# Pair 7's transposes in the other half of a PSUM pair, eight slices of an output tile ahead of pair 6's second scores, and nine more fixed orders, in a cosine attention with a gated product behind it

## The chip, the cores and the metric

The kernel runs on one core of a Trainium2 chip. Its engines are TensorE (PE, the matmuls), VectorE (DVE), ScalarE (ACT), GpSimd (POOL) and SyncE (SP, which here only issues transfers). Each engine works through its own list of instructions in order and waits at semaphores for the others. The metric is the device time in microseconds (us), the median of some runs. Beside it stands one profiled execution, whose rows give each instruction's start and length counted from the start of its span.

## The reference

The inputs are `q`, `k` and `v` of shape (8, 12, 448, 64): batch, heads, positions, width of a head; then `w_in` (768, 2048) and `w_out` (2048, 768), and the scale `tau` = 0.1. Cut to what matters:

```python
q_n = q / (norm(q, axis=-1) + 1e-06)
k_n = k / (norm(k, axis=-1) + 1e-06)
scores = q_n @ k_n.T / tau                       # 448 x 448 for each batch and head
attn = exp(scores - max); attn = attn / (sum(attn) + 1e-09)
attn_out = attn @ v
x = attn_out.transpose(0, 2, 1, 3).reshape(3584, 768)
h = x @ w_in                                     # 3584 x 2048
g = h * cos(h)
out = g @ w_out                                  # 3584 x 768
```

## The kernel before

**How the work is cut.** Two heads make a *pair* `g` (48 of them), three pairs a *unit* `u` (16), two units a batch `b` (8). Six pairs give the 768 columns of `x` for one batch of 448 rows.

For a unit, `load` brings q and k. `square` (`sq4.2` is unit 4, pair 2 of the unit) and `reduce` (`red4.2`, on DVE) give squared norms, `rnorm` their inverse roots, `scale` the normalised q and k in `qks`. `transposes(g)` turns them into `qkT`. From pair 9 on that is a transposing transfer issued on SP (`T39` is pair 39's). Before that it is seven PE transposes in two parts (`TP6`), written to PSUM, and one DVE copy (`qkT6`, L716). There are three `qkT` buffers.

`scores(g, c)` computes one of four chunks (`SC7.1` is pair 7, chunk 1; chunk 0 is half as long as the others) into `SC1` for even c and `SC0` for odd c, and ACT takes the exponential into `PX` (`exp7.1`, L742). So a score has to wait until the exponential two chunks earlier has emptied its buffer. `attend` multiplies by v into the PSUM pair AV (`AV7`, with a rest `R7` for the half chunk). Row sums come from ones in the same product for the "direct" pairs (among them 7 to 11 and 17), or for the others from `counts` (`S6`, L788), which marks the sums into AV; a DVE copy (`xs2`) and a small chain of transfers (gather, reciprocal, spread, bcast) bring the inverse sums back. `xa` and `xb` are the DVE copies that empty AV. The last step for a pair is `x7`, the product with the inverse sums, on POOL for all pairs from 6 on.

With a batch's six pairs in `xT`, `m1(b)` computes h in 16 passes of six matmuls (`M1 0.13` is batch 0, pass 13, L953). Two passes fill one PSUM pair; ACT takes the cosine (`sin0.6`, L982) and DVE the product (`g0.6`, L984) into `gT`. The cosine and the exponential need different ACT tables, so a table load (L556) stands between. For batch 0 the eight pairs of passes go to the PSUM pairs MP, SC1's pair, SC0's, AV and so on by `"first": (3, 1, 2, 0, 3, 1, 2, 0)`, counted in AV, SC0, SC1, MP. Passes 8 and 9 are thus in MP, 12 and 13 in the PSUM pair `SC[1]`, 14 and 15 in AV.

The second product works on output tiles of 128 rows (28 of them). Its units here are *slices*: one slice takes 128 of the 2048 inner columns for half of the 768 output columns; a tile has 32. While attention still runs, a slice is done as four 64 by 64 matmuls into both halves of MP (`m2_quarters`, L1053). The first tile takes its slices in runs (0 to 8, 8 to 12, 12 to 16, each with both crossings, `"cuts": (8, 12)`), and a run on the other crossing waits until the last has drained. Slices 0 to 7 need the parts W2.0 and W2.1 of `w_out`, 8 to 11 W2.2, 12 to 15 W2.3. `osb10` is the copy of tile 10 out of PSUM, by DVE for one half and ACT for the other, and `out10` its store.

**The halves of MP.** The PSUM pair MP has two banks: the lower is `TP` (and `TPF` for the second product), the upper `PO` or, in bfloat16, `POT`. In `transposes`, pairs in `PLAN["other"]` would use `POT`; the others use `TP`.

**How the pairs and the second product are woven.** `pair(g, f)` issues pair g's four scores, pair g-1's attend, and between them slices of the second product, as many as the four numbers `f` say: `f[0]` after the first score, `f[1]` and `f[2]` around the third, `f[3]` after the fourth. Pair 6 takes `f` from `PLAN["six"]`; the others from `PLAN["given"]` where they stand there, or from `shares`. For pairs whose predecessor is in `PLAN["quarters"]`, `f[1]` stands before the attend of that predecessor.

**What sets the order.** Each step is an `Op` with an engine, what it reads and writes, and a cost that the plan assumes. `Program.arrange` (L152) plays the list three times: PE keeps nearly the order written (it may pick among the next 8, or 24 at the start), the other engines pick, of what is ready, the step with the earliest due time, worked back from when PE needs it. `emit` (L315) then writes each engine's list with its waits. Near the end of the program `PLAN["then"]` is read (L1326):

```python
for x, y in PLAN["then"]:
    P.order_only([o for o in P.ops if o.label == x and o.eng == find(y).eng][-1], find(y))
```

which makes step y stand behind step x on y's engine. It adds no wait between engines.

Of the kernel before, what the change touches and what calls it, by code (L numbers as in the profile page):

```python
# [35 lines left out]
    "split5at": 0,  # L36
    "wait6": 1,
    "b5": -5.0,
    "then": [('g5.0', 'recip12'), ('g5.6', 'red15.2'), ('osb10', 'ln11.0'), ('xa32', 'red12.1'), ('sq12.2', 'x29'), ('g5.7', 'red15.2'), ('xa37', 'red14.1'), ('sq7.1', 'scale6.1'), ('g2.7', 'red9.1'), ('T20', 'out4')],
    "u7": (None, None, None),  # L40
    "v6": "sq5.1",
    "yield": {},
# [7 lines left out]
    "turned": 9,  # L50
    "first": (3, 1, 2, 0, 3, 1, 2, 0),
    "inner": {6: (6, 7), 7: (8,)},
    "other": (),
    "bs": -1.0,
    "cuts": (8, 12),
    "bx": 0.0,
    "six": (0, 8, 4, 4),
    "cycle": {13: 3, 14: 3, 15: 3, 16: 3, 17: 3, 18: 3, 46: 3, 47: 3},
    "quarters": (7, 8, 9, 10, 11, 17),
    "turns": {3: (3, 0, 1, 2, 0, 1, 2, 0)},  # L60
# [5 lines left out]
    "u5": ("gather2", "gather2", "gather2"),  # L66
    "tail": 192,
    "twin": 4,
    "given": {13: (0, 0, 3, 3), 16: (5, 1, 3, 6), 22: (0, 3, 5, 6), 26: (3, 2, 5, 6), 27: (0, 0, 3, 2), 34: (12, 4, 5, 6), 46: (12, 4, 4, 5), 47: (3, 1, 5, 0), 14: (4, 0, 3, 3), 15: (3, 1, 4, 2), 17: (2, 1, 3, 4), 18: (3, 0, 3, 4), 19: (6, 4, 2, 7), 20: (0, 5, 5, 3), 21: (3, 5, 3, 6), 23: (4, 1, 5, 5)},
    "roots": (3, (8, 0), (10, 0), (12, 0), (14, 0)),  # L70
    "lead": {33: 5, 45: 5, 12: 13, 21: 13},
    "vloads": {3: [(4, "x6"), (5, "x6")], 4: [], 5: [], 6: [(7, "x15"), (8, "x15")], 7: [], 8: [], 9: [], 10: [], 11: [], 12: [], 13: []},
# [1292 lines left out]
```

## Time and profile before

| | |
|---|---|
| median of 3 runs | 415.38 us (415.3 to 415.99) |
| the profiled execution | 415.07 us, span 413.2 us |
| PE busy | 404.6 us (98%) |
| ACT busy | 270.2 us (65%) |
| POOL busy | 248.6 us (60%) |
| DVE busy | 199.8 us (48%) |
| granted TensorE clock | 1.0 of full speed |

The span is the time from the first to the last profiled instruction; the execution's own time is 1.9 us longer. In a row of the timeline the first number is the start and the second the length, then engine, line, operation, what is written from what is read, and the count; in square brackets stands the idle time of the engine before it and who ended it. Matmuls overlap, so a row of several can be longer than its share of PE's time, and the distance between starts tells the work.

### The profile page before, as it was taken

What the parts mean: (1) busy time and instruction counts of PE and PEld (TensorE: products, weight loads), DVE (VectorE), ACT (ScalarE), POOL (GpSimd) and SP (SyncE); (2) the same over time, 40 slices, a digit from 0 to 9 for tenths busy, and PEclk for the clock granted to TensorE, in tenths of its full rate; (3) what the DMA queues carried; (4) which work ended last, traced back from release to release, by engine and by line L of the source; (5) the groups of instructions that cost most, each with busy time, mean ns of one, the idle gap of its engine ahead of it and who ended that gap; (6) DMA issues with size and microseconds to landing.
All of it is one profiled execution on the core that took longest, in us unless ns stands there. A gap on an engine that the chain in (4) does not pass through costs nothing.

```text
span 413.2 us, 13911 instructions
## 1 busy us (share of the span) xinstructions
PE 404.6 (98%) x6213; PEld 244.0 (59%) x6213; DVE 199.8 (48%) x279; ACT 270.2 (65%) x384; POOL 248.6 (60%) x196
## 2 busy tenths in 40 slices
PE   7899999999999999999999999999999999999997
PEld 3454556655566655765567656865567655655565
DVE  4574653426664457445644567344652344413421
ACT  4897578985889645985497647884488745623500
POOL 4999995894776975988589756946456303011000
PEclk9999999999999999999999999999999999999999
DMA  8999999589989999587978975797746531151023
GB/s 183 249 254 226 207 223 200 134 158 215 180 147 171 234 260 189 98 195 182 208 120 189 250 128 110 137 236 167 104 89 108 147 84 33 47 139 38 2 74 80
DMA packets 78736, 63.99 MB, mean 155 GB/s; under 512 B 41844, under 2 KB 72404, under 8 KB 78676
## 3 DMA queue, kind: packets, MB, share of 16 engines
q1 hardware_dynamic: 60468, 50.42, 55.0%
q0 software_dynamic: 18048, 12.59, 20.8%
q8 instruction: 49, 0.80, 0.8%
q10 hardware_dynamic: 160, 0.10, 0.1%
q14 instruction: 11, 0.09, 0.1%
HBM read 55.44 MB, written 11.19 MB: 161 GB/s over the span
## 4 chain that ended last, share of the span: by engine, by line
PE 91%; POOL 3%; ACT 2%; DVE 2%; DMA 1%; issue 0%; SPq 0%; ACTq 0%; POOLq 0%
PE MP L1053 27%; PE SC L953 20%; PE AV L953 12%; PE SC L727 6%; PE AV L764 5%; PE MP L1082 4%; PE AV L788 4%; PE SC L1082 3%; PE MP L953 2%; PE AV L837 2%; POOL qks L678 1%; PE SC L735 1%; ACT cosb L982 1%; PE MP L852 1%; PE AV L1082 1%; DMA raw<-in_q_dram 1%
## 5 line engine op out<-in xcount | busy, mean ns | idle before, releaser
L742 ACT ACTIVATE PX<-SC 128x448 bf16<-128x448 f32 (+1 forms) x192 | 148.9, 825 | 15.9 <-PE SC L727 10.5
L1053 PE MATMUL MP<-W,gT 64*64 64x384 bf16 x2816 | 136.6, 323 | 0.8 <-DVE qkT L716 0.6
L1053 PEld LDWEIGHTS MP<-W,gT 64*64 64x64 bf16 x2816 | 80.0, 107 | 34.9 <-issue 4.4
L953 PE MATMUL SC<-xT,W 128*128 128x448 bf16 x444 | 90.9, 353 | 0.0
L678 POOL TENSOR_TENSOR qks<-raw,rn 128x896 bf16<-128x896 f32 (+1 forms) x48 | 79.9, 1677 | 13.0 <-ACT rn L670 12.6
L640 POOL TENSOR_TENSOR sq<-raw 128x896 bf16<-128x896 f32 x44 | 74.0, 1687 | 12.4 <-DMA raw<-in_q_dram 7.7
L940 POOL TENSOR_TENSOR xT<-xu,RB 128x448 bf16<-128x448 f32 x36 | 40.2, 1136 | 66.1 <-DMA RB<-scr 66.1
L953 PEld LDWEIGHTS SC<-xT,W 128*128 128x128 bf16 x444 | 43.1, 98 | 40.2 <-issue 0.4
L982 ACT ACTIVATE cosb<-SC,cst 128x896 f32<-128x896 f32 x37 | 37.2, 1006 | 37.8 <-PE SC L953 35.9
L953 PE MATMUL AV<-xT,W 128*128 128x448 bf16 x276 | 59.6, 352 | 0.0
L984 DVE TENSOR_TENSOR gT<-SC,cosb 128x896 bf16<-128x896 f32 x37 | 40.3, 1089 | 29.2 <-ACT cosb L982 29.1
L647 DVE TENSOR_REDUCE n<-sq 128x14 f32<-128x896 bf16 (+2 forms) x49 | 51.4, 1058 | 6.1 <-ACT sq L638 4.9
L727 PE MATMUL SC<-qkT 64*64 64x448 bf16 x576 | 51.9, 354 | 0.3
L982 ACT ACTIVATE cosb<-AV,cst 128x896 f32<-128x896 f32 x23 | 23.2, 1007 | 37.1 <-PE AV L953 35.4
L774 DVE COPY xu<-AV 128x448 f32<-128x448 f32 x36 | 22.5, 624 | 49.1 <-PE AV L756 49.1
L953 PEld LDWEIGHTS AV<-xT,W 128*128 128x128 bf16 x276 | 26.6, 98 | 25.4 <-DVE xs L799 1.1
L984 DVE TENSOR_TENSOR gT<-AV,cosb 128x896 bf16<-128x896 f32 x23 | 25.1, 1089 | 27.4 <-ACT cosb L982 27.4
L764 PE MATMUL AV<-PX,va 64*64 64x448 bf16 x432 | 38.2, 349 | 0.0
L614 POOL DMA_DIRECT2D va<-in_v_dram x32 | 22.0, 694 | 24.8 <-DVE gT L984 20.2
L1019 DVE COPY osb<-MP 128x384 f32<-128x384 f32 x26 | 14.5, 557 | 43.1 <-PE MP L1053 32.0
L727 PEld LDWEIGHTS SC<-qkT 64*64 64x64 bf16 x576 | 16.8, 106 | 12.8 <-ACT PX L742 5.9
L775 DVE TENSOR_TENSOR xu<-xu,AV 128x448 f32<-128x448 f32 x36 | 22.3, 621 | 1.2
(84 smaller groups left out, 364.1 us busy)
## 6 DMA issues: line engine op xcount, KB each, us to landing
raw<-in_k_dram SPq DMA_DIRECT2D x48, 224.0 KB, 5.2
raw<-in_q_dram SPq DMA_DIRECT2D x48, 224.0 KB, 5.6
out_dram<-osb SPq DMA_DIRECT2D x54, 192.0 KB, 3.4
RB<-scr SPq DMA_DIRECT2D x22, 336.0 KB, 5.3
va<-in_v_dram POOLq DMA_DIRECT2D x32, 192.0 KB, 6.9
W<-in_moe_w_in_dram POOLq DMA_DIRECT2D x4, 768.0 KB, 14.8
W<-in_moe_w_out_dram POOLq DMA_DIRECT2D x4, 768.0 KB, 18.9
qkT<-qks SPq DMA_TRANSPOSE x39, 3.8
```

The lines of the kernel that those rows point to most:

```text
L640: pool(lambda e, x=x, y=y: e.tensor_tensor(y, x, x, ALU.mult), src_, dst, 0.1 + n * 1.78e-3, label="sq%d.%d" % (u, p)).pad = LATE if u > 1 ...
L647: dve(lambda e, w=w: e.tensor_reduce(out=n2v[i][:, 2 * p : 2 * p + 2, w], in_=sqv[p][:, :, w, :], axis=mybir.AxisListType.X, op=ALU.add), ...
L678: f = lambda e, s0=s0, s1=s1: e.tensor_tensor(qksv[i][:, p, s0:s1].rearrange("p s h d -> p h s d"), rawv[i][:, h, s0:s1, :], bass.AP(rn[i] ...
L727: m = e.matmul(SCv[z][BP * o : BP * o + BP, a, 0:S], t[r, c - 1 + (NT3 + 1) * o, 0:BP], t[r, :, BP : 2 * BP], start=True, stop=True)
L742: act(lambda e: e.activation(PHv[j] if c == 0 else PXv[j][:, c - 1], SCv[z][:, :, 0:n], ACT.Exp, scale=1.0 / TAU), ["SC%d" % z], [("PX", j ...
L764: m = e.matmul(AVv[64 * a : 64 * a + 64, o, 0:S], vav[y][r, 2 * p + a, c + 1, :], PXv[j][r, c, a, :], start=(c == 0), stop=False)
L940: f = lambda e, p=p: e.tensor_tensor(xTv[b % 2][:, UP * i + p, :].rearrange("p (s o m) -> p o s m", s=NB, o=2), xuv[:, u % 3, p, :].rearra ...
L953: t = e.matmul(ph[:, a, 0:S], W1v[:, order[c], 128 * n : 128 * n + 128], xTv[b % 2][:, order[c], :], start=(c == 0), stop=(c == NKC - 1))
L982: act(lambda e, ph=ph, cz=cz: e.activation(cosv[cz], ph[:, :, 0:S], ACT.Sin, bias=cst.ap()[:, 0:1], scale=1.0), names(gi) + ["cst0"], [("c ...
L984: dve(lambda e, ph=ph, cz=cz, gi=gi: e.tensor_tensor(gTv[:, 2 * gi : 2 * gi + 2, S * (b % 2) : S * (b % 2) + S], ph[:, :, 0:S], cosv[cz], ...
L1053: r = e.matmul(POH[b][x : x + 64, 0:HW], gTv[k, y, col + x : col + x + 64], W2v[k, y, HW * b : HW * b + HW], start=(y == 0 and h == 0), st ...
L1082: r = e.matmul(po[:, 0 : w[1] - w[0]], gTv[:, y, col : col + 128], W2v[:, y, w[0] : w[1]], start=(y == 0), stop=(y == NF - 1))
```

## The change

Four entries of `PLAN` change, and no code.

```diff
-    "then": [('g5.0', 'recip12'), ..., ('T20', 'out4')],
+    "then": [('g5.0', 'recip12'), ..., ('T20', 'out4'), ('x8', 'sq4.2'), ('xa12', 'red6.0'), ('g4.7', 'red13.2'), ('osb10', 'red11.2'), ('osb16', 'red14.2'), ('spread11', 'T39'), ('osb11', 'red12.0'), ('xa15', 'red7.0'), ('g5.4', 'red15.1')],
...
-    "other": (),
+    "other": (7,),
...
-    "six": (0, 8, 4, 4),
+    "six": (8, 8, 4, 0),
...
-    "given": {13: (0, 0, 3, 3), ...},
+    "given": {7: (0, 0, 3, 4), 13: (0, 0, 3, 3), ...},
```

The first adds nine orders: seven on DVE, one on POOL (`x8` before `sq4.2`), one on SP (`spread11` before `T39`). The second puts pair 7's transposes in `POT`. The third moves eight slices of the first output tile from behind pair 6's second score to behind its first, and takes the four behind its fourth away (with the run of eight, sixteen slices now stand before the third score, where eight stood). The fourth fixes pair 7's slices, which `shares` gave before.

The list that the plan makes of it differs in these places. PE, from the transposes of pair 6 to the second score of pair 8:

```
before: TP6, M1 0.13, M1 0.14, TP7, M1 0.15, TP8, SC6.0, SC6.1, 8 slices, SC6.2, 4, SC6.3, 4, AV6, SC7.0, AV6, SC7.1, AV6, R6, SC7.2, 4, SC7.3, 1, S6, 3, SC8.0, 4, SC8.1, 4
after:  TP6, TP7, M1 0.13, TP8, M1 0.14, M1 0.15, SC6.0, 8 slices, SC6.1, 8, SC6.2, 4, SC6.3, AV6, 3, SC7.0, AV6, 1, SC7.1, AV6, SC7.2, R6, 4, SC7.3, 2, S6, SC8.0, 2, SC8.1
```

Further on PE has the same order, but for the first partial passes of `M1 5`, where passes 2 and 3 (in SC0) now both stand ahead of 0 and 1 (in AV). On DVE the copies `qkT7` and `qkT8` stand ahead of `g0.6`, and the seven reductions behind their new partners. On ACT `osb0` stands ahead of `exp8.1`, `expS7`, `rn4.0`, `expS10` and `ln4.1` a few places later. On POOL W2.1 is issued ahead of the load of v for unit 2, W2.2 ahead of `sq3.0`; `x7` stands behind `scale4.0`, `sq4.2` behind `x8`, `x6` behind `x10`, one load of v further back, and `sq12.1` ahead of `scale12.0`. On SP `T11` stands ahead of the last load of unit 4 and the first of unit 5, and `out14` and `spread11` ahead of `T39`.

More of the change, by code (lines that the diff above doesn't have):

```diff
@@ L38 @@
     "b5": -5.0,
-    "then": [('g5.0', 'recip12'), ('g5.6', 'red15.2'), ('osb10', 'ln11.0'), ('xa32', 'red12.1'), ('sq12.2', 'x29'), ('g5.7', 'red15.2'), ('xa37', 'red14.1'), ('sq7.1', 'scale6.1'), ('g2.7', 'red9.1'), ('T20', 'out4')],
+    "then": [('g5.0', 'recip12'), ('g5.6', 'red15.2'), ('osb10', 'ln11.0'), ('xa32', 'red12.1'), ('sq12.2', 'x29'), ('g5.7', 'red15.2'), ('xa37', 'red14.1'), ('sq7.1', 'scale6.1'), ('g2.7', 'red9.1'), ('T20', 'out4'), ('x8', 'sq4.2'), ('xa12', 'red6.0'), ('g4.7', 'red13.2'), ('osb10', 'red11.2'), ('osb16', 'red14.2'), ('spread11', 'T39'), ('osb11', 'red12.0'), ('xa15', 'red7.0'), ('g5.4', 'red15.1')],
     "u7": (None, None, None),
@@ L68 @@
     "twin": 4,
-    "given": {13: (0, 0, 3, 3), 16: (5, 1, 3, 6), 22: (0, 3, 5, 6), 26: (3, 2, 5, 6), 27: (0, 0, 3, 2), 34: (12, 4, 5, 6), 46: (12, 4, 4, 5), 47: (3, 1, 5, 0), 14: (4, 0, 3, 3), 15: (3, 1, 4, 2), 17: (2, 1, 3, 4), 18: (3, 0, 3, 4), 19: (6, 4, 2, 7), 20: (0, 5, 5, 3), 21: (3, 5, 3, 6), 23: (4, 1, 5, 5)},
+    "given": {7: (0, 0, 3, 4), 13: (0, 0, 3, 3), 16: (5, 1, 3, 6), 22: (0, 3, 5, 6), 26: (3, 2, 5, 6), 27: (0, 0, 3, 2), 34: (12, 4, 5, 6), 46: (12, 4, 4, 5), 47: (3, 1, 5, 0), 14: (4, 0, 3, 3), 15: (3, 1, 4, 2), 17: (2, 1, 3, 4), 18: (3, 0, 3, 4), 19: (6, 4, 2, 7), 20: (0, 5, 5, 3), 21: (3, 5, 3, 6), 23: (4, 1, 5, 5)},
     "roots": (3, (8, 0), (10, 0), (12, 0), (14, 0)),
```

## The prediction

> **What bounds the kernel now.** I read the page first (engine totals), then busy time by stage, then the timelines of PE, ACT and DVE around pair 6, where the change cuts, then the transfers that land there.
>
> ```profile
> span 413.2 us, 13911 instructions
> PE 404.6 (98%) x6213; PEld 244.0 (59%) x6213; DVE 199.8 (48%) x279; ACT 270.2 (65%) x384; POOL 248.6 (60%) x196
> ```
> ```profile
> 50.67:65.96 15.29, 14.43 (x257) 8.66 (x258) 7.85 (x11) 11.14 (x15) 12.28 (x10) 1.00 1.18 214
> 65.96:106.50 40.54, 40.54 (x632) 23.93 (x624) 19.03 (x23) 32.14 (x48) 28.68 (x23) 1.00 0.90 177
> 106.50:143.00 36.50, 36.40 (x895) 23.81 (x891) 19.65 (x30) 32.61 (x52) 28.92 (x21) 1.00 0.90 179
> 143.00:373.00 230.00, 229.91 (x3754) 142.57 (x3753) 112.68 (x145) 146.60 (x197) 133.72 (x102) 1.00 0.72 146
> ```
>
> In the stage rows the number before the comma is the stretch, the one behind it PE's busy time. From 65.96 to 373 PE lacks 0.19 us of 307. From 50.67 to 65.96, between the transposes of pair 6 and the third scores of pair 8, it lacks 0.86. TensorE is the bound, and of the middle of the kernel only this stretch has idle time to give. Its rows:
>
> ```profile
> 50.67 0.55 PE L702 MATMUL MP<-ident,qks 128*128 128x128 bf16 x7
> 51.06 1.30 PE L953 MATMUL SC<-xT,W 128*128 128x448 bf16 x6
> 53.34 0.55 PE L702 MATMUL MP<-ident,qks 128*128 128x128 bf16 x7
> 53.73 1.30 PE L953 MATMUL AV<-xT,W 128*128 128x448 bf16 x6
> 55.18 0.56 PE L702 MATMUL MP<-ident,qks 128*128 128x128 bf16 x7 [0.16 <-DVE qkT L716]
> 55.67 0.29 PE L735 MATMUL SC<-qkT 64*64 64x224 bf16 x4
> 55.80 0.36 PE L727 MATMUL SC<-qkT 64*64 64x448 bf16 x4
> 56.79 1.50 PE L1053 MATMUL MP<-W,gT 64*64 64x384 bf16 x32 [0.64 <-DVE qkT L716]
> 58.09 0.39 PE L727 MATMUL SC<-qkT 64*64 64x448 bf16 x4
> 58.35 0.84 PE L1053 MATMUL MP<-W,gT 64*64 64x384 bf16 x16
> ...
> 60.47 0.38 PE L727 MATMUL SC<-qkT 64*64 64x448 bf16 x4
> ...
> 62.37 0.57 PE L788 MATMUL AV<-PX,mark 128*32 128x224 bf16 x16
> 62.86 0.68 PE L1053 MATMUL MP<-W,gT 64*64 64x384 bf16 x12
> 63.37 0.27 PE L735 MATMUL SC<-qkT 64*64 64x224 bf16 x4
> 63.71 0.84 PE L1053 MATMUL MP<-W,gT 64*64 64x384 bf16 x16
> ...
> 65.96 0.36 PE L727 MATMUL SC<-qkT 64*64 64x448 bf16 x4
> ```
> ```profile
> 52.46 1.01 ACT L982 ACTIVATE cosb<-SC,cst 128x896 f32<-128x896 f32 x1 [1.65 <-DVE qkT L716]
> 55.12 1.01 ACT L982 ACTIVATE cosb<-AV,cst 128x896 f32<-128x896 f32 x1 [1.65 <-DVE qkT L716]
> 56.15 1.28 ACT L556 ACT_TABLE_LOAD   x1
> 57.44 6.00 ACT L742 ACTIVATE PX<-SC 128x448 bf16<-128x448 f32 x8
> ```
> ```profile
> 51.85 0.61 DVE L716 COPY qkT<-MP 128x896 bf16<-128x896 bf16 x1
> 53.50 1.09 DVE L984 TENSOR_TENSOR gT<-SC,cosb 128x896 bf16<-128x896 f32 x1 [1.04 <-ACT cosb L982]
> ...
> 62.98 0.39 DVE L799 COPY xs<-AV 128x224 f32<-128x224 f32 x1 [0.52 <-PE AV L788]
> ```
>
> The rows of seven are TP6, TP7 and TP8, all in the lower half of MP: each waits for the copy (L716) of the one before. Row 55.18 shows TP8 held by TP7's copy, row 56.79 the first output tile held by TP8's. Matmuls overlap, so I take work as start to start. Two passes of six matmuls are 51.06 to 53.34, so 1.14 a pass and 0.19 a matmul (four small ones side by side take the same). A set of transposes is 53.34 to 53.73, 0.39; a turn of the array to another tiling 0.10 (55.18 to 55.67 is 0.49); eight slices of an output tile 1.30 (56.79 to 58.09), 0.163 each; a half score 0.10; the counts with their turn 0.49 (62.37 to 62.86). A slice that begins a new run onto the other bank waits 0.07 more for the last to drain (58.09 to 58.35). By that measure three waits stand here: before TP8 55.18 - 53.73 - 1.14 = 0.31; before the tile 0.99 - 0.19 = 0.80; before 63.71 0.34 - 0.10 = 0.24, that drain with too little between. On ACT the eight exponentials of pairs 6 and 7 run without a gap for 6.00.
>
> **The change, part by part.** No work is added or removed: the same matmuls, copies and transfers in another order.
>
> *Transposes.* TP7 goes to MP's upper half, so TP6 and TP7 stand at 50.67 and 51.06, M1 0.13 at 51.45, TP8 at 52.59 (TP6's copy ends at 51.85 + 0.61 = 52.46, just in time), M1 0.14 at 52.98, M1 0.15 from 54.12 to 55.26. The 0.31 goes, since a whole pass lies between TP6's copy and TP8. But M1 0.15 stands one set of transposes later, 54.12 for 53.73. What is late next is ACT: its last cosine moves from 55.12 to 55.51, the table load ends at 57.82, the exponentials start 0.39 later, and their eighth ends at 63.83 where it ended at 63.44.
>
> *First score.* It needs bank SC1, which g0.6 frees, and g0.6 now stands behind all three copies on DVE. M1 0.13 ends at 51.45 + 1.30 = 52.75, its cosine runs 52.85 to 53.86 (row 52.46 starts 0.10 after its pass), the product (1.09) to 54.98; TP8's copy is over by 53.8. PE arrives at 55.36: no wait.
>
> *Eight slices ahead of the second score.* They start at 55.46 and not at 56.79, the copies being long done: the 0.80 goes. Then, by the durations above: SC6.1 56.76; eight slices 57.02 to 58.32; SC6.2 58.42 (exp6.0, half a chunk, 0.54, ends at 58.37); four slices 58.7; SC6.3 59.35; AV6 59.54; three slices to 60.22; SC7.0; AV6 60.31; one slice; SC7.1 waits for exp6.3 until 60.86, 0.20 lost; SC7.2 for exp7.0 until 61.37, 0.13 lost; R6 61.56; four slices 61.67 to 62.32; SC7.3; two slices 62.6; counts 63.0; SC8.0 63.5; two slices 63.7; SC8.1 64.05 (exp7.3 is over at 63.83); AV7 64.24 (the counts' copy ends at 63.0 + 0.57 + 0.05 + 0.39 = 64.01); SC8.2 64.91. Against row 65.96 that is **1.05 us gained**. The same from the other side: 0.31, 0.80 and 0.17 of the 0.24 go; 0.33 of waits on ACT come, of which some 0.1 stood before row 60.47 already: 1.05. A cap: SC8.1 cannot pass 63.88, nor SC8.2 64.74, so no more than 1.2.
>
> The sum hangs on ACT starting its exponentials straight behind the table load: row 56.15 ends at 57.43, row 57.44 follows 0.01 later. A drain between them as long as the load itself (1.28) would undo the gain, 415.4 to 415.6; the row speaks against it. [...]
>
> *Weights of the second product.* On POOL's queue W2.1 goes ahead of v of unit 2, W2.2 ahead of a square; W2.3 stays last, with the same bytes ahead of it. The tile now asks for W2.3 (slices 12 to 15) after R6, at 61.67, before at 63.71.
>
> ```profile
> L1107 POOL DMA_DIRECT2D W<-in_moe_w_out_dram x1: 803/803/803, 42.0 to 42.0; - x1
> DMA to landing us min/median/max: 18.5/18.5/18.5
> ```
> ```profile
> DMA to landing us min/median/max: 15.7/18.9/20.5
> ```
>
> Issued at 42.0 it lands at 60.5, 1.2 us ahead. All four W2 transfers (last row) took 15.7 to 20.5, so 57.7 to 62.5 bounds it: a wait of 0.8 at worst. I take its own value: no wait.
>
> *The nine orders.* Seven put a DVE copy or product ahead of a norm reduction that ran in time when the copy had to wait anyway. The dearest place is osb10:
>
> ```profile
> 211.22 1.08 DVE L647 TENSOR_REDUCE n<-sq 128x14 f32<-128x896 bf16 x1
> 212.97 0.56 DVE L1019 COPY osb<-MP 128x384 f32<-128x384 f32 x1 [0.68 <-PE MP L1053]
> 213.95 0.62 DVE L774 COPY xu<-AV 128x448 f32<-128x448 f32 x1 [0.41 <-PE AV L756]
> ```
> ```profile
> 216.61 0.36 PE L764 MATMUL AV<-PX,va 64*64 64x448 bf16 x4
> ```
>
> osb10 waits 0.68 for PE either way, so nothing is won; the reduction now ends near 214.5 and pushes xa28 by 0.5, and with it xb28 (0.62 more), to 215.75: 0.85 before PE takes AV again at 216.61. Zero; the bounds are a loss and a gain of 0.5 a place. On POOL x8 goes ahead of sq4.2, on SP T39 behind out14 and spread11:
>
> ```profile
> 82.85 1.13 POOL L907 TENSOR_TENSOR xT<-xu,RB 128x448 bf16<-128x448 f32 x1
> ```
> ```profile
> 85.86 1.31 PE L953 MATMUL MP<-xT,W 128*128 128x448 bf16 x6
> ```
> ```profile
> 268.01 1.62 SPq L695 DMA_TRANSPOSE qkT<-qks  x1
> ```
> ```profile
> 276.24 0.27 PE L735 MATMUL SC<-qkT 64*64 64x224 bf16 x4
> ```
>
> x10 ends at 83.98 and is read at 85.86. The square (about 1.7, as its neighbours) now comes before it and x6 (about 1.1) after it: some 0.5 later, 1.3 still spare. T39's scores come 8.2 after its issue; two short issues pass it. T11 moves ahead of the last loads of unit 4 and must wait for pair 8's scores, which holds them some 4 us; their first user, sq4.2, has itself moved that far. The last M1 pass of batch 5 opens its SC banks before AV. All zero.
>
> **Sum.** 1.05 less on the span, 412.2, and on the profiled execution, 415.07, gives 414.0; that execution lies 0.31 under the median of 415.38. **Forecast 414.3.**
>
> **The rivals.**
> *ACT becomes the bound of the stretch.* For it: the exponentials start 0.39 later, and in my walk SC6.2 has 0.05 to spare and SC7.1 and SC7.2 wait. If five of the six scores from SC6.2 to SC8.1 slip by 0.1 more, the gain is 0.55: 414.8. Against: any slip before exp7.3 that PE can fill with slices is not lost.
> *Slower: W2.3 lands late.* PE then stands in front of the last eight slices, with pairs 7 and 8 queued behind. Each us after 61.67 costs one; from 62.7 the gain is gone, from 63.6 (21.6 after issue) it is slower by over 0.2%; at 22 it is 416.6. Against: no W2 transfer took over 20.5. For: equal sizes spread over 4.8 us, and W2.3 is still in flight while SP issues other loads. [...]
> *The gain is made and given back.* A later wait is set by a transfer, or a pin pushes a copy into PE's way (0.5 each): 415.1 to 415.6. Against: the stage rows show PE without a gap, so what follows moves with it.
> *More than forecast:* no wait on ACT, and a pin that helps: 413.9.
>
> **How the numbers follow.** No change means within 0.2%, 0.83 us, about what a measurement of this kernel can tell: 414.55 to 416.21. Forecast case 0.57 (gain 0.7 to 1.2), more 0.08, ACT 0.12, given back 0.12, W2.3 or another late transfer 0.10, a drain behind the table load 0.01. Faster: most of the forecast case (0.49), all of "more", a quarter of ACT's: 0.60. Slower: the late transfer and a third of "given back", 0.14. Same: 0.26. Range 413.8 to 415.6; the likeliest case alone 413.9 to 414.8 with the scatter of runs.
>
> **What would show it.** TP6 and TP7 back to back; no idle time before TP8 nor before the tile's first slices; the table load ending 0.4 later; short waits at SC7.1 and SC7.2; SC8.2 about 1.05 earlier, and the same distance kept at 106 and at 373. I am wrong if slices stand waiting for W2.3, if the first score waits for g0.6, or if the distance shrinks at a pinned place.

## The result and the profile after

The changed kernel takes 414.8 us (median of 22 runs, 413.88 to 416.63) beside 415.37 of the kernel before in the same measurement (median of 22, 414.9 to 416.76). The ratio is 0.9982 with a 95% interval of 0.9974 to 0.9991: faster by 0.57 us in the medians, by 1.02 between the fastest runs. Forecast were 414.3 and a range of 413.8 to 415.6. The runs of after spread more: their fastest lies 0.92 under their median, before's 0.47.

The execution of after that was profiled is one of the long ones, 416.12 us. Its page begins:

```profile
span 414.3 us, 13911 instructions
PE 405.4 (98%) x6213; PEld 244.4 (59%) x6213; DVE 199.9 (48%) x279; ACT 269.7 (65%) x384; POOL 248.6 (60%) x196
```

That span is 1.1 us *longer* than before's 413.2. Two things are in it, and they are told apart by following one mark through the kernel. The first is the timeline of PE around pair 6 (start, length, operation, idle time before it):

```profile
50.69 0.94 PE L702 MATMUL MP<-ident,qks 128*128 128x128 bf16 x14
51.47 1.30 PE L953 MATMUL SC<-xT,W 128*128 128x448 bf16 x6
52.61 0.55 PE L702 MATMUL MP<-ident,qks 128*128 128x128 bf16 x7
53.00 2.43 PE L953 MATMUL AV<-xT,W 128*128 128x448 bf16 x12
55.36 0.29 PE L735 MATMUL SC<-qkT 64*64 64x224 bf16 x4
...
56.78 0.36 PE L727 MATMUL SC<-qkT 64*64 64x448 bf16 x4
57.02 1.49 PE L1053 MATMUL MP<-W,gT 64*64 64x384 bf16 x32
58.44 0.38 PE L727 MATMUL SC<-qkT 64*64 64x448 bf16 x4
...
60.87 0.38 PE L727 MATMUL SC<-qkT 64*64 64x448 bf16 x4
61.09 0.36 PE L764 MATMUL AV<-PX,va 64*64 64x448 bf16 x4
61.31 0.38 PE L727 MATMUL SC<-qkT 64*64 64x448 bf16 x4
61.52 0.27 PE L756 MATMUL AV<-PX,va 64*64 64x224 bf16 x4
61.62 0.82 PE L1053 MATMUL MP<-W,gT 64*64 64x384 bf16 x16
...
63.90 0.38 PE L727 MATMUL SC<-qkT 64*64 64x448 bf16 x4
...
64.77 0.36 PE L727 MATMUL SC<-qkT 64*64 64x448 bf16 x4
```

TP6 and TP7 are one row of 14 without a break; no row from TP8 to the first slices has idle time; and the third score of pair 8 stands at 64.77 where it stood at 65.96. That is 1.19 us gained in this stretch. ACT's timeline of the same stretch:

```profile
55.53 1.01 ACT L982 ACTIVATE cosb<-AV,cst 128x896 f32<-128x896 f32 x1 [1.65 <-PE AV L953]
56.55 1.28 ACT L556 ACT_TABLE_LOAD   x1
57.85 6.50 ACT L742 ACTIVATE PX<-SC 128x448 bf16<-128x448 f32 x9
```

Everything on it moved 0.4 later, and the exponentials begin 0.02 behind the end of the table load.

The second is a stop of PE 52 us later. PE's timeline there, and its list of waits for the whole kernel (us in total, times, longest):

```profile
116.19 0.36 PE L764 MATMUL AV<-PX,va 64*64 64x448 bf16 x4
116.38 0.33 PE L1053 MATMUL MP<-W,gT 64*64 64x384 bf16 x3
118.32 0.51 PE L1053 MATMUL MP<-W,gT 64*64 64x384 bf16 x5 [1.61 <-issue]
118.51 0.51 PE L727 MATMUL SC<-qkT 64*64 64x448 bf16 x4
```
```profile
PE MP L1053 <- issue: 1.6, 1, 1.6
```

PE stops for 1.61 us between the third and the fourth matmul of a run of slices. Both have the same kind of operands, all long there; the profile names no engine and no transfer as releaser, only "issue". Up to 116.38 the kernel ran 1.19 us ahead of before; behind the stop it is 0.62 late. That is where the profiled execution lost more than it had won: 1.8 us by the starts, a little more than the idle time in the row: the three matmuls ahead of it stand there with 0.33, where three of these take 0.12 from start to start (32 in 1.30, 56.79 to 58.09 before). A second stop of the same kind at 283 takes 0.4 more, and the execution ends 1.08 behind.

What PE may have lacked is found among the transfers. The page counts among the DMA queues one named `q8 instruction`, with 49 packets of together 0.80 MB, so 16 KB each; PE's 12,426 matmuls and weight loads make about 254 a packet, or 256 with the 128 semaphore and drain instructions recorded on its list. From this fit I take the packets to be PE's own program; the page does not say which engine a packet is for. Transfers of after in the stretches 112 to 115 and 115.9 to 116.9 us, by queue (packets, MB, share of the engines' time):

```profile
q1 hardware_dynamic: 520, 0.80, 105.7%
```
```profile
DMA packets 24, 0.02 MB, mean 24 GB/s; under 512 B 22, under 2 KB 23, under 8 KB 23
q1 hardware_dynamic: 23, 0.01, 13.8%
q8 instruction: 1, 0.02, 5.9%
```

In the first stretch the data transfers alone (loads of q, a transpose, an output) fill the engines (the times of packets overlap, as the share of 105.7% shows) and no instruction packet moves. In the second one packet does; by its record it starts at 115.93 and has landed at 116.88. PE stands from about 116.7 and goes on at 118.32, 1.44 us behind the landing. How many instructions PE began meanwhile is shown by the busy time between the packets' starts, in after and then in before (columns: stretch; its length; busy time and count on PE, PEld, DVE, ACT and POOL; granted clock; DMA share; GB/s):

```profile
108.09:115.93 7.84, 7.84 (x212) 5.49 (x208) 5.99 (x9) 7.60 (x13) 4.84 (x4) 1.00 1.17 162
115.93:120.07 4.14, 2.53 (x60) 1.56 (x52) 0.36 (x2) 1.40 (x3) 4.14 (x3) 1.00 0.70 162
```
```profile
108.66:114.00 5.34, 5.34 (x132) 3.37 (x132) 3.52 (x6) 5.26 (x9) 5.21 (x4) 1.00 0.58 140
```

Before, the twelfth packet started some 264 instructions of PE (132 and 132) behind the eleventh. In after it started some 420 behind it (212 and 208), a DMA share of 1.17 standing between them. (Instructions at the edge of a stretch are counted in both.) The granted clock is 1.00 throughout.

### The profile page after: what moved, and what is told of

The parts are those of the page before. It is cut to its first block, busy times and chain, and to the rows that moved or that the text cites. A ratio compares the mean times of both kernels' runs of the same rounds, so it can differ in the third digit from the quotient of the medians.

```text
span 414.3 us, 13911 instructions
## 1 busy us (share of the span) xinstructions
PE 405.4 (98%) x6213; PEld 244.4 (59%) x6213; DVE 199.9 (48%) x279; ACT 269.7 (65%) x384; POOL 248.6 (60%) x196
## 2 busy tenths in 40 slices
DMA packets 78736, 63.99 MB, mean 154 GB/s; under 512 B 41844, under 2 KB 72404, under 8 KB 78676
## 4 chain that ended last, share of the span: by engine, by line
PE 93%; POOL 3%; ACT 2%; DMA 1%; issue 1%; DVE 0%; SPq 0%; ACTq 0%; POOLq 0%
PE MP L1053 27%; PE SC L953 20%; PE AV L953 13%; PE SC L727 7%; PE AV L764 5%; PE MP L1082 4%; PE AV L788 4%; PE SC L1082 3%; PE MP L953 2%; PE AV L837 2%; POOL qks L678 1%; PE SC L735 1%; PE MP L852 1%; PE AV L1082 1%; DMA raw<-in_q_dram 1%; PE AV L828 1%
```

## The experiments

Two accounts were tested. One: the gain of about 1.1 us is there in every execution, and part of it is taken back by stops that come by chance, when a packet of instructions is late among crowded data transfers. The other: one of the parts of the change, the nine orders above all, brings the later loss. The kernels were timed beside the kernel before on the same chip, whose medians were 414.98 (first four), 415.04 (next four) and 415.02 (last two). Kernels reach pair 6 up to 0.2 us earlier or later than before does (one of them 0.65 later), so besides the place of pair 8's third score the length of the stretch is given, from the start of TP6 to that score: 15.29 before (50.67 to 65.96), 14.08 after (50.69 to 64.77).

### The change once more

No edit.

> The changed kernel once more, unaltered. Theory 1 (the gain of the stretch is there in each execution, and what takes it back is a chance stop of PE, in which its own instructions come late): the third scores of pair 8 stand near 64.8 us again, 1.1 to 1.2 ahead of before; a stop of 1.6 us need not stand at 116.7 again; the fastest execution lies about 1.0 under the fastest of before, the median 0.4 to 1.0 under. Theory 2 (the new orders themselves make the loss at 116.7): the stop stands at the same place with the same 1.6 us, and the distance to before at 120 us is again a loss of about 0.7.

Measured: 414.25 (413.64 to 415.57, 12 runs), ratio 0.9981 (0.9971 to 0.9992). The profiled execution has the third score of pair 8 at 64.67 and no stop at 116, but one in a first-product pass:

```profile
187.26 1.11 PE L953 MATMUL AV<-xT,W 128*128 128x448 bf16 x5
188.87 0.35 PE L953 MATMUL AV<-xT,W 128*128 128x448 bf16 x1 [0.50 <-issue]
```

The stretch takes 14.08 again; the stop is at another place and shorter. What stands at 116 in the first profile is therefore no property of the new order.

### The stretch without the nine orders

```diff
     "other": (7,), "six": (8, 8, 4, 0), "given": {7: (0, 0, 3, 4), ...},   # as after
-    "then": [..., ('T20', 'out4'), ('x8', 'sq4.2'), ...],
+    "then": [..., ('T20', 'out4')],
```

> The transposes of pair 7 in the other half, and the slices of pairs 6 and 7, without the nine orders. Theory 1: the same 1.1 to 1.2 us at pair 8's third scores, and a median 0.4 to 1.0 under before, like the changed kernel. Theory 2 (the orders cost): better than the changed kernel by 0.5 or more.

Measured: 414.09 (413.69 to 415.94, 12 runs), ratio 0.9982 (0.9971 to 0.9994); third score of pair 8 at 64.76, the stretch 14.08 long; no stop in its profile, whose span is 412.1, 1.1 under before's. In this execution nearly the whole gain reaches the end with all transfers in place.

### The nine orders alone

```diff
     "then": [..., ('x8', 'sq4.2'), ..., ('g5.4', 'red15.1')],   # as after
-    "other": (7,),  "six": (8, 8, 4, 0),  "given": {7: ..., 13: ...},
+    "other": (),    "six": (0, 8, 4, 4),  "given": {13: ...},
```

> The nine orders alone. Theory 1: the third scores of pair 8 stay at 65.9 to 66.0, the median within 0.3 of before. Theory 2: slower than before by 0.4 or more, with an idle time of PE behind a pinned place or near 116 us.

Measured: 415.18 (414.77 to 415.92, 11 runs), ratio 1.0004 (0.9996 to 1.0013). The third score of pair 8 stands at 65.94, and the tile keeps its wait:

```profile
56.77 1.49 PE L1053 MATMUL MP<-W,gT 64*64 64x384 bf16 x32 [0.64 <-DVE qkT L716]
```

The two kernels together: the orders cost nothing and bring nothing that can be measured (the interval runs from 0.2 us faster to 0.5 slower), and the whole gain is in the stretch, 15.29 long here.

### Pair 7's transposes alone

```diff
     "other": (7,),
-    "then": [..., ('x8', 'sq4.2'), ...],  "six": (8, 8, 4, 0),  "given": {7: ..., 13: ...},
+    "then": [..., ('T20', 'out4')],       "six": (0, 8, 4, 4),  "given": {13: ...},
```

> Only the other half of MP for pair 7's transposes; the slices stay behind the second score of pair 6. Theory 1, if the place of TP7 makes the gain: no idle time before TP8 nor before the tile's first slices, pair 8's third scores at 64.8 to 65.1, median 0.4 to 1.0 under before. If the slices ahead of the second score make it (rival): PE waits for ACT where they now stand, the third scores come at 65.3 or later, and the median is within 0.4 of before.

Measured: 414.61 (414.0 to 415.94, 12 runs), ratio 0.9989 (0.9979 to 0.9999). The third score of pair 8 is at 64.96, 1.0 ahead of before; but TP6 starts at 50.54 in this profile, so the stretch is 14.42 long and 0.87 of it is gained. Both waits went: the second score now stands straight behind the first, and sixteen slices follow without idle time. What it lacks shows at the fourth score:

```profile
55.52 3.04 PE L1053 MATMUL MP<-W,gT 64*64 64x384 bf16 x64
58.38 0.36 PE L727 MATMUL SC<-qkT 64*64 64x448 bf16 x4
59.10 0.38 PE L727 MATMUL SC<-qkT 64*64 64x448 bf16 x4 [0.35 <-ACT PX L742]
```

PE has run out of slices in front of it and waits for ACT's exponential. The new distribution of slices avoids that wait, and the stretch is 0.34 shorter with it (14.08). The 0.2 between the two places of the score (64.96 and 64.76) understates this, since the two kernels enter the stretch 0.14 apart.

### The slices alone

```diff
     "six": (8, 8, 4, 0),  "given": {7: (0, 0, 3, 4), ...},
-    "other": (7,),  "then": [..., ('x8', 'sq4.2'), ...],
+    "other": (),    "then": [..., ('T20', 'out4')],
```

> Only the slices of pairs 6 and 7 as in the change; pair 7's transposes stay in the lower half of MP. If the place of TP7 makes the gain: the first slices still wait for TP8's copy, the idle 0.6 us stays, pair 8's third scores at 65.6 to 66.1, median within 0.3 of before. If the slices make it: pair 8's third scores at 65.3 or earlier, and 0.4 or more under before.

Measured: 415.26 (414.62 to 415.9, 11 runs), ratio 1.0002 (0.9993 to 1.001). Both waits stand as they stood:

```profile
54.96 0.56 PE L702 MATMUL MP<-ident,qks 128*128 128x128 bf16 x7 [0.16 <-DVE qkT L716]
...
56.57 1.49 PE L1053 MATMUL MP<-W,gT 64*64 64x384 bf16 x32 [0.64 <-DVE qkT L716]
```

The third score of pair 8 stands at 65.56, a little earlier than expected, but TP6 starts at 50.45, 0.22 ahead of before. The stretch is 15.11 long: the slices alone win 0.18. What goes is the wait in front of the run of slices behind pair 8's first score (63.73 to 63.82, before 63.37 to 63.71). Otherwise eight slices ahead of the second score are worth nothing as long as the copy of pair 8's transposes, at the end of the row of three copies through one half of MP, holds back the tile. So the 0.80 that I had put under the slices is won by the place of TP7; 0.87 and 0.18 alone make 1.05, both together 1.21.

### Can the late packet be moved?

Three kernels tried to set where a packet is late, by the transfers of SP's queue. The first moves one load of unit 11 away from the packet that was late in the repeat (at 186):

```diff
+    for x, y in (('load u11 p0', 'out9'),):
+        find(x).start = find(y).start + 1e-6
```

> The changed kernel with one move on SP's queue alone: the first load of unit 11 (448 KB, issued near 181 us between bcast7 and out8) goes behind out9. Theory (PE's own instructions come in 16 KB packets through the same DMA engines, and in a full stretch a packet is late; the packet near 187 us was late in all six profiles so far, begun 349 to 433 instructions after its turn where 160 to 300 is usual, and at over 425 PE stopped): the packet near 186 us begins at 300 or under, no stop of PE at M1 3, the middle of the runs 0.1 to 0.4 under the changed kernel's. Rival (the stops have nothing to do with the transfers): the packet stays late and the times are the changed kernel's within 0.1.

Measured: 415.01 (414.31 to 415.8, 12 runs), ratio 0.9997 (0.9988 to 1.0006). The packet near 186 is on time and there is no stop there, as expected, but the gain does not come, and the median is back at before's: the next packet but one is late instead, under the moved load, and PE stops there. (In this profile the granted clock was 0.97 in the first 64.7 us, and TP6 starts at 51.32, which puts the third score of pair 8 at 65.40; the stretch is 14.08 long.)

```profile
212.46 0.36 PE L764 MATMUL AV<-PX,va 64*64 64x448 bf16 x4
213.57 0.38 PE L727 MATMUL SC<-qkT 64*64 64x448 bf16 x4 [0.75 <-issue]
```

The second does the reverse. It adds a transfer of 917 KB that nothing needs, in front of the same packet:

```diff
+    o = dma("SP", [... q into an unused buffer, 128 x 1792 f32 ...], [], [], "junk", 2.0, "load junk")
+    o.start = o.end = find("out8").start + 1e-6
```

> The changed kernel with one transfer more on SP's queue, behind out8 near 182 us: 917 KB from q to a scratch tensor that nobody reads; no engine's list changes otherwise. Theory: the instruction packet near 187 us comes later still and PE stops in M1 3 for 1 to 4 us without waiting for any step; the median is 1 to 4 us over the changed kernel's. Rival (no tie between transfers and PE's instructions): no such stop; at most a late load, whose users have some 10 us to spare, so within 0.3 of the changed kernel.

Measured: 414.01 (413.64 to 415.63, 12 runs), ratio 0.9978 (0.9968 to 0.9988). The stop that was expected did not come, and the kernel is no slower than the change. The packet near 186 starts at position 381 (positions are explained with the table below), no later than in the change (381 and 431). The heavy transfer in the same stretch did not make the packet later here. PE does wait once for data in this profile, 0.36 at 132, for a transposing transfer.

The third is the stretch alone with that load of unit 11 and one of unit 7 moved, to keep the packets at 116 and at 186 on time:

```diff
+    for x, y in (('load u11 p0', 'out9'), ('load u7 p2', 'gather4')):
+        find(x).start = find(y).start + 1e-6
```

> The transposes and slices without the nine orders, with two loads moved back on SP's queue: the first load of unit 11 behind out9, the third of unit 7 behind gather4 (from the stretch at 110 to 117 us, where the changed kernel's profile had its stop). Theory: both late packets go, the stretch's 1.1 us stays, and the median comes to 1.0 under before (413.9 to 414.1), with fewer executions near 415. Rival: as the changed kernel, 0.7 under before.

Measured: 414.68 (414.19 to 415.6, 12 runs), ratio 0.9994 (0.9985 to 1.0003). Both packets are on time, and as before a third one is late, with a stop of 0.5 at 212. The expectation of 413.9 to 414.1 failed, and a better version than the change was not found this way.

### The same kernels with less to load

To see the stretch without stops, both kernels were run with a quarter of the rows of q and k loaded from unit 6 on; the rest of the input is left out, so their results are not the reference's:

```diff
-        return bass.AP(t.tensor, ..., [[NB * D, BP], [S * D, nh], [1, NB * D]])
+        return bass.AP(t.tensor, ..., [[NB * D, 16 if u >= 6 else BP], [S * D, nh], [1, NB * D]])
...
-            rawv[i][BP * x : BP * x + BP, h]...
+            rawv[i][BP * x : BP * x + (16 if u >= 6 else BP), h]...
```

> The kernel before, in which the loads of q and k for units 6 to 15 bring 16 of 64 rows of partitions (the rest keeps what units 4 and 5 left there); every list and every wait is the same. It leaves out three quarters of those transfers, about 26 of the 64 MB. Theory (chance stops of PE, each ending some 1.4 us after a packet of PE's instructions that came late in crowded DMA engines): no stop over 0.3 us behind 70 us, the middle of its executions close to its fastest, 414.6 to 415.0. Rival (the stops have another cause): spread and median as before, 415.0.

> The changed kernel with the same transfers left out (16 of 64 rows of partitions of q and k for units 6 to 15). Theory: no stop over 0.3 us behind 70 us, and the whole gain of the stretch stands in the median: 1.0 to 1.2 under the kernel before with the same transfers left out. Rival (the gain is given back by the order, not by late packets): the difference stays at 0.6 to 0.8.

Measured: the kernel before so lightened 414.89 (414.71 to 415.15, 11 runs), ratio to before 0.9995 (0.9986 to 1.0004); the changed one 413.69 (413.55 to 414.37, 5 runs), ratio to before 0.9966 (0.9952 to 0.9979). What is left out is less than expected: 53.67 MB are moved for 63.99, so about 10 MB less and not 26. PE's busy time between 66 and 373 us, in before, after, the repeat of after, the light before and the light after (columns as above):

```profile
66.00:373.00 307.00, 306.81 (x5275) 190.29 (x5264) 151.32 (x196) 211.31 (x296) 191.32 (x145) 1.00 0.76 154
```
```profile
66.00:373.00 307.00, 304.98 (x5241) 189.52 (x5230) 151.00 (x195) 210.42 (x295) 190.18 (x144) 1.00 0.78 154
```
```profile
66.00:373.00 307.00, 306.32 (x5247) 189.81 (x5240) 150.78 (x195) 210.31 (x295) 191.45 (x145) 1.00 0.77 155
```
```profile
66.00:373.00 307.00, 306.81 (x5272) 190.52 (x5265) 151.28 (x196) 211.31 (x296) 190.45 (x145) 1.00 0.62 121
```
```profile
66.00:373.00 307.00, 306.81 (x5252) 190.28 (x5245) 150.85 (x195) 210.60 (x295) 191.34 (x145) 1.00 0.61 121
```

With the DMA share at 0.62 and 0.61 neither profile has an idle row of this kind, and PE lacks 0.19 us in both; the two profiles of the change lack 2.02 and 0.68. (Four of the ten other profiles, at shares of 0.75 to 0.78, have no such row either, so its absence alone proves little.) The medians of the light kernels lie 1.20 apart, their third scores of pair 8 1.00 (65.89 and 64.89). The light changed kernel enters the stretch 0.21 later than the light before, so the stretch itself gives 1.21 (15.29 and 14.08). Taking data away from the DMA engines hardly helped the kernel before (414.89 beside 415.02). The changed one took 414.80 and 414.25 with all data and takes 413.69 here, but it was not run with all data in this measurement, so the 0.6 to 1.1 between them compares different measurements. This is what the first account asks for: nearly the whole gain of the stretch reaches the end when hardly a packet costs time. It is shown for these medians; with five runs of the light changed kernel their spread is known only roughly.

### All stops of all profiles

Each stop of this kind between 66 and 373 us, with the record of its packet. The position is how many recorded instructions of its list PE had begun (matmuls, weight loads and semaphore instructions), less 256 for each packet sent earlier; a packet usually starts at 160 to 310.

| kernel | packet starts, lands (us) | position at its start | PE goes on (us) | position of the stop |
|---|---|---|---|---|
| after | 115.93, 116.88 | 430 | 118.31 | 449 |
| after | 280.49, 281.75 | 309 | 283.22 | 449 |
| the repeat | 186.45, 187.53 | 431 | 188.87 | 449 |
| transposes alone | 186.90, 187.99 | 433 | 189.45 | 449 |
| one load moved | 210.95, 212.13 | 372 | 213.57 | 449 |
| two loads moved | 209.53, 210.88 | 355 | 212.21 | 449 |
| slices alone | 230.59, 231.92 | 348 | 233.23 | 449 |
| slices alone | 280.15, 281.24 | 317 | 282.70 | 449 |

The last column is the evidence for the cause. All eight stops, in four different kinds of work and at times from 116 to 283 us, come at the very same place counted in instructions: a whole number of packets, of 256 each, apart in PE's list. From this I conclude that PE had run out of its program there; no row shows what it still held. The last column but one, beside the landings, shows that PE went on 1.31 to 1.47 us behind them.

The packets that cost nothing fit as well. The twelve profiles hold 504 packets between 66 and 373 us, and in no case does PE begin the instruction behind position 449 less than 1.23 us after the landing; the eight stops lie at 1.31 to 1.47. Four smaller losses lie at the same position, at 1.23 to 1.46, and show in the starts but in no idle row: beside before's starts PE falls back by 0.28 near 118 with the nine orders alone, 0.29 near 117 with one load moved, 0.27 near 233 with the transfer added, and 0.10 near 276 in the light kernel after. So kernels without a row in the table lost time at that position too, the nine orders alone among them, which leave the stretch as it was.

Not every late packet cost something, and how fast PE goes through its list has to do with it: in 64 x 64 slices it begins about 50 instructions a microsecond (32 matmuls and as many weight loads in 1.30, 56.79 to 58.09 before), in 128-wide passes about 10 (6 and 6 in 1.15, 187.41 to 188.56 before). Before's own packet at 187.18 started at position 421 without a stop: it fell into such passes, where by my estimate from that rate the 28 instructions to 449 take 2.7 us, and it had landed after 1.11.

## Why the prediction was right, and where not

*Transposes: right.* TP8 was put at 52.59 and stands at 52.61, without a wait; ACT's last cosine, the end of the table load and the exponentials were put 0.39 later and are 0.40 to 0.41 later.

*First score: right.* No wait for `g0.6`; 55.36 forecast, 55.36 found.

*Eight slices: right in the walk, wrong in which part earns it.* Second score 56.76 forecast, 56.78 found; third 58.42 and 58.44; fourth 59.35 and 59.33; the second of pair 7 60.86 and 60.87, with the short wait for ACT in front of it; the third of pair 7 61.37 and 61.31. The 0.80 before the tile goes, but the run with the slices alone shows that it stays without the place of TP7, and the run with the transposes alone that the slices add 0.34 by avoiding a wait for ACT. The sum is right, its division between the two parts is not.

*W2.3: right.* The slices that need it start at 61.62 without idle time. W2.3 was issued at 41.9 and took 19.0, so it landed at 60.9, where 60.5 was forecast.

*Nine orders: right.* Alone they measure 1.0004, and the kernel with them and the one without them have the same time within their intervals (414.25 and 414.09).

*No drain behind the table load: right.* 56.55 + 1.28 = 57.83, first exponential 57.85; and the cosine ahead of the load ends at 55.53 + 1.01 = 56.54, 0.01 before it. The forecast gave a drain behind the table load a chance of 0.01; no run shows one: the first exponential follows the load's end by 0.01 in before and with the transposes alone, by 0.02 in after.

*Size of the stretch: 1.05 forecast, 1.19 found, the cap being 1.2.* The term that was too dear is the step from the first to the second score of pair 8. I counted 0.55 for the score, the turn and two slices, with a drain in it; 63.46 to 63.90 is 0.44. The rest, 0.04, is there already at pair 8's first score (63.46 for 63.5).

*The sum of the whole: too high a gain.* 0.57 (here) and 0.73 (in the repeat) for 1.05 forecast. The step that failed is "what follows moves with it, the same distance kept at 106 and at 373". At 106 it was kept (1.19). It was kept to the end in the profile without the nine orders (1.15) and, but for 0.10, in the light kernels; in the profiled execution it broke at 116. The stage rows had shown me PE without a gap in one execution, and I took that for a property of the kernel; it is one of that execution as well. So the rival "made and given back" came true in part, but not through what I named: in the two profiles of the change no wait was set by a transfer of data, and no order pushed a copy into PE's way. What gave it back there were the stops at position 449, 1.31 to 1.47 us behind the landing of a packet, by my reading PE's own program arriving late: a cost that my sum does not have. That the medians lie in the middle of the range, and not at the forecast, is most likely the weight of these stops; for the medians this rests on the light kernels, since each kernel has one profiled execution.

Two things in the forecast need a word more. I had called everything within 0.2% of before "no change", with a chance of 0.26, and 0.57 us is 0.18%: by that line the result is no change, though its interval excludes zero. And 414.8 is the very time that I gave the rival in which ACT becomes the bound. That is chance: its five slipping scores did not come, and the stretch gained the full 1.19.

*Left open.* Whether the change makes stops more frequent than they were. Median less fastest is 0.92 and 0.61 in the two measurements of after, 0.40 for the stretch without the orders, 0.61 for the transposes alone, and 0.29 to 0.47 for before; that points to it, but the slices alone have 0.64 without the gain and the change with the transfer added 0.37, and an accidental meeting of transfers and packets would look the same. A lower clock is not behind the spread: of the 22 runs of the change one had a mean granted clock under 0.999, 0.996, and it took 414.86. And what exactly makes a packet late: moving a load moved the late packet on, adding a load did nothing.

## What to carry to other kernels

When several results go through one buffer, ask which one ends the queue: giving the middle of three the other half of the buffer freed the last (0.87 us), and the reordered work behind it picked up the rest (0.34). The gain on the bounding engine in the middle of this long unrolled program was kept where no stop stood behind an instruction packet (1.20 between the medians of the light kernels), and one such stop took more than all of it (1.8 us at 116 for 1.19); where a trace shows idle time that nothing released, in the middle of a run of equal instructions, look for the instruction queue among the transfers before blaming the new order. Compare the fastest runs too: here they differ by the full step of the stretch (1.02), the medians by half of it.

## What the hardware showed unexpectedly

Between the data stand the packets of 16 KB on the queue `q8 instruction`, 49 of them in before and in after, each 0.88 to 1.81 us long, which makes one for some 256 instructions on PE's list. With the DMA share of a stretch at 1.17 one started some 420 instructions after its predecessor, where in before it is 264. PE stopped at the same count of instructions each time, 449 by the table, for up to 1.61 us, and went on 1.31 to 1.47 us after the landing. That it had none of its program left there is a conclusion from this fixed count; no run shows how much PE can hold. Of the 504 packets of the twelve profiles eight stand at a stop and four at a smaller loss. At DMA shares of 0.61 and 0.62 between 66 and 373 us the largest loss was 0.10, at 0.75 to 0.79 it went from nothing to 1.8 us.
